# Every fp32r matmul reads and writes its 512 columns in pairs, by turns from the two halves of the row

## The chip, the core and the metric

The kernel runs on one core of a Trainium2 chip. TensorE (PE) multiplies, VectorE (DVE) and ScalarE (ACT) do the elementwise work, GpSimd (POOL) and SyncE (SP) mostly issue DMAs. The time is that of the whole program on the device, in microseconds (us).

## The reference

One transformer block with an FNet mixing layer and a feed-forward layer, S = 2048 rows, D = 512, F = 1792, all fp32:

```python
def _A_ref(x, dft_seq_re, dft_seq_im, dft_hid_re, dft_hid_im):
    a = jnp.einsum("bsd,ed->bse", x, dft_hid_re)
    b = jnp.einsum("bsd,ed->bse", x, dft_hid_im)
    return jnp.einsum("ts,bse->bte", dft_seq_re, a) - jnp.einsum("ts,bse->bte", dft_seq_im, b)

def _B_ref(x, w1, w2):
    h = _silu(jnp.einsum("bsd,df->bsf", x, w1))
    return jnp.einsum("bsf,fd->bsd", h, w2)

h = x + _A_ref(_layernorm(x), ...)
out = h + _B_ref(_layernorm(h), w1, w2)
```

## The kernel before

Every product is made of fp32r matmuls. An fp32 operand is rounded into a high part (on ScalarE, line 266) and a remainder (on VectorE, line 270 or 272), and one product of a weight block with a moving row takes three matmuls: high by high, high by remainder, remainder by high. That is the function `three`, lines 314 to 318. Each of these matmuls loads 128x128 weights, streams 512 moving columns past them and adds the 128x512 result to half of a double PSUM bank (`banks`, two rows of 512 fp32). The moving operand is always one row of 512 fp32r per partition, the high or the low half of a page in SBUF.

The stages, in order: `plain` (the first sequence products, with `L513`, `L515` and `L517` for the first quarter, where the three kinds of matmul are grouped over four blocks), `fast` (the other sequence products, in Strassen-Winograd form with seven products per 2x2 blocks), `mix_fast` (the hidden products), `up` (first feed-forward matrix, with SiLU behind it) and `down` (second feed-forward matrix). Tiles are called ph and pl (parts of the sequence matrices and of mixed blocks), X and S (parts of the normalized input and its sums, which are the weights of the first stages), T1 to T7, gth and gtl (parts of activations), hf, sf, wf, wah, wal (weights).

The order of all instructions is written out ahead of time: each piece of work is an event with a planned time (`step` for matmuls, `at` for others), shifted by a table `MOVED`, and the sorted list fixes the order on every engine. The plan counts `MM_US = 0.2265` for a matmul, prepares remainders `PREP_US = 8` us and loads tiles `LOAD_US = 18` us ahead of their matmul; the waits themselves are semaphores, so that a plan which is off moves the order and not what waits for what. Twelve bf16 matmuls (line 1357) warm TensorE up at the start. They are written apart from `three`.

Of the kernel before, what the change touches and what calls it, by code (L numbers as in the profile page):

```python
# [206 lines left out]
def fnet_ffn_kernel(  # L207
# [18 lines left out]
    for plan.now, *_, f in program(stub, plan.page, stub, stub, stub, stub, x, xT, seq, hid, ffn, out):  # L226
        f()
    places = plan.places()

    def page(name, dt=F32, shape=(2, 512)):  # L230
        return pages.tile([P, *shape], dt, tag=f"pg{next(places)}", name=name)

    events = program(nc, page, keep, small, psum, dram, x, xT, seq, hid, ffn, out)


# [12 lines left out]
def program(nc, page, keep, small, psum, dram, x, xT, seq, hid, ffn, out):  # L248
# [11 lines left out]
    def banks(name):  # L260
        return psum.tile([P, 2, 512], F32, tag="ps", name=name)
# [43 lines left out]
    def newton(v, t, a, b):  # L305
# [5 lines left out]
            nc.vector.tensor_tensor(v, v, t, op=ALU.mult)  # L311
        nc.vector.scalar_tensor_tensor(b, v, 1.5, a, op0=ALU.add, op1=ALU.mult)

    def three(acc, wh, wl, mh, ml, first, last, on=False):

        nc.tensor.matmul(acc, wh, mh, start=first, stop=False, skip_group_check=on)  # L316
        nc.tensor.matmul(acc, wh, ml, start=False, stop=False, skip_group_check=on)  # L317
        nc.tensor.matmul(acc, wl, mh, start=False, stop=last, skip_group_check=on)  # L318

    events, clock = [], [0.0]  # L320

# [116 lines left out]
    raw, part, acc, C = {}, {}, {}, {}  # L438
# [56 lines left out]
    def plain(c, q):  # L495


        def mul(jj, k, tau, tiles, parts):
            hi, lo = parts
            if not acc:  # L500
                for v in ((1, 1), (0, 0), (1, 0), (0, 1)):
                    acc[c, q, *v] = banks(f"c{c}{q}{v[0]}{v[1]}")
            for a in tiles:
                todo = []
                for i in range(2):
                    w = X[i, k, jj]
                    for m in range(2):
                        d = slice(m * P, (m + 1) * P)
                        todo.append((acc[c, q, i, tau][:, m, :], w[:, 0, a, d], w[:, 1, a, d], hi[:, a, :], lo[:, a, :]))
                first, last = jj == 0 and k == 0 and a == 0, jj == 1 and k == 1 and a == 1  # L510
                if jj == 0 and tau == 0:
                    for o, wh, _, mh, _ in todo:
                        nc.tensor.matmul(o, wh, mh, start=first, stop=False)  # L513
                    for o, wh, _, _, ml in todo:
                        nc.tensor.matmul(o, wh, ml, start=False, stop=False)  # L515
                    for o, _, wl, mh, _ in todo:
                        nc.tensor.matmul(o, wl, mh, start=False, stop=last)  # L517
                else:
                    for v in todo:
                        three(*v, first, last)  # L520
# [22 lines left out]
        for a in range(2):  # L543
            step(24, lambda a=a: [mul(0, 0, tau, [a], part[key]) for tau, key in enumerate(keys)])
# [32 lines left out]
        for jj, k, tau in [(jj, k, tau) for jj in range(2) for k in range(2) for tau in range(2)][2:]:  # L577
            key = ("A", c, q, jj, k, tau)
            before = [(LOAD_US, lambda jj=jj, k=k, tau=tau, key=key: load_seq(c, q, jj, k, tau, key)),
                      *halves(PREP_US, lambda key=key: round_raw(key))]  # L580
            if k == 0 and tau == 0:
                before += tiles_x(jj)
            after = [(0, lambda: copy_out("22", acc.pop((c, q, 1, 1))))] if (jj, k, tau) == (1, 1, 1) else []
            step(24, lambda jj=jj, k=k, tau=tau, key=key: mul(jj, k, tau, (0, 1), part.pop(key)), before, after)
# [5 lines left out]
        def prod(n, jj):  # L590
            hi, lo = part.pop(("A", c, q, n, jj))
            w = X[(*A[n], jj)]
            if (n, jj) in ((1, 2), (7, 2)):
                acc[n] = banks(f"c{n}")
            o = acc[{2: (c, q, 0, 0), 3: (c, q, 0, 1), 4: (c, q, 1, 0), 7: 7}.get(n, 1)]
            fresh = n in (1, 7)
            for m in range(2):
                for a in range(2):
                    d = slice(m * P, (m + 1) * P)
                    three(o[:, m, :], w[:, 0, a, d], w[:, 1, a, d], hi[:, a, :], lo[:, a, :],  # L600
                          fresh and jj == 2 and a == 0, jj == 3 and a == 1, not fresh)
# [62 lines left out]
    def fast(c, q):  # L664
# [4 lines left out]
        def mul(n, jj, on=False):  # L669
            hi, lo = part.pop(("A", c, q, n, jj))  # L670
            w = X[(*A[n], jj)]
            for m in range(2):
                for a in range(2):
                    d = slice(m * P, (m + 1) * P)
                    three(acc[c, q, n][:, m, :], w[:, 0, a, d], w[:, 1, a, d], hi[:, a, :], lo[:, a, :],
                          jj == JJ[0] and a == 0 and not on, jj == JJ[-1] and a == 1, on)
# [717 lines left out]
```

## Time and profile before

| | |
|---|---|
| median of 3 runs | 666.58 us (666.52 to 734.88) |
| the profiled execution, its own time | 665.71 us |
| its span, first to last instruction | 663.9 us |
| PE busy, matmuls | 657.9 us, 2892 |
| VectorE busy | 575.6 us |
| ScalarE busy | 371.7 us |
| DMA | 184.22 MB, mean 277 GB/s |

Times in the profile are from the span's start. PE is the stream of matmuls, PEld the weight loads, which run beside it. Matmuls overlap each other (the next one starts while the last columns of the one before are still on their way), so the busy time of one says less than the distance from start to start. PEclk is the clock granted to TensorE, in tenths of full speed. A line like `4.89 0.81 PE L1357 ... x3` in the timeline is a start, the time from the first start to the last end, and how many instructions were put together.

### The profile page before, as it was taken

What the parts mean: (1) busy time and instruction counts of PE and PEld (TensorE: products, weight loads), DVE (VectorE), ACT (ScalarE), POOL (GpSimd) and SP (SyncE); (2) the same over time, 40 slices, a digit from 0 to 9 for tenths busy, and PEclk for the clock granted to TensorE, in tenths of its full rate; (3) what the DMA queues carried; (4) which work ended last, traced back from release to release, by engine and by line L of the source; (5) the groups of instructions that cost most, each with busy time, mean ns of one, the idle gap of its engine ahead of it and who ended that gap; (6) DMA issues with size and microseconds to landing.
All of it is one profiled execution on the core that took longest, in us unless ns stands there. A gap on an engine that the chain in (4) does not pass through costs nothing.

```text
span 663.9 us, 8288 instructions
## 1 busy us (share of the span) xinstructions
PE 657.9 (99%) x2892; PEld 541.9 (82%) x2892; DVE 575.6 (87%) x727; ACT 371.7 (56%) x476; POOL 99.4 (15%) x131
## 2 busy tenths in 40 slices
PE   9999999999999999999999999999999999999997
PEld 5888888888888888888888888888888888888885
DVE  7999989898988999989999998988998854379974
ACT  6997456664445435365674555778543555664600
POOL 0011011112003433111121005343010000000000
PEclk9999999999999999999999999999999999999999
DMA  8982899999799586999999987668979663278803
GB/s 324 370 224 48 269 353 370 313 298 302 268 363 364 165 295 127 397 330 397 322 323 412 408 321 270 237 222 315 342 276 376 226 227 118 80 258 305 324 32 128
DMA packets 59706, 184.22 MB, mean 277 GB/s; under 512 B 6800, under 2 KB 13840, under 8 KB 59664
## 3 DMA queue, kind: packets, MB, share of 16 engines
q1 hardware_dynamic: 45024, 131.22, 54.9%
q0 software_dynamic: 14352, 52.20, 24.6%
q8 instruction: 23, 0.38, 0.3%
q10 hardware_dynamic: 288, 0.26, 0.1%
q14 instruction: 19, 0.16, 0.1%
HBM read 139.34 MB, written 44.32 MB: 277 GB/s over the span
## 4 chain that ended last, share of the span: by engine, by line
PE 98%; DMA 0%; DVE 0%; ACT 0%; issue 0%; DVEq 0%
PE m L318 11%; PE m L316 11%; PE m L317 11%; PE y L318 8%; PE y L317 8%; PE y L316 8%; PE f L318 6%; PE f L317 6%; PE f L316 6%; PE c L317 4%; PE c L316 4%; PE c L318 4%; PE vx L318 3%; PE vx L317 3%; PE vx L316 3%; PE c L517 1%
## 5 line engine op out<-in xcount | busy, mean ns | idle before, releaser
L266 ACT ACTIVATE ph<-raw 128x1024 fp32r<-128x1024 f32 x102 | 106.0, 1057 | 86.7 <-PE m L318 18.6
L270 DVE TENSOR_TENSOR pl<-raw,ph 128x1024 fp32r<-128x1024 f32 x88 | 112.1, 1289 | 8.9 <-ACT ph L266 6.8
L316 PE MATMUL m<-ph,S 128*128 128x512 f32 x192 | 74.7, 389 | 0.0
L317 PE MATMUL m<-pl,S 128*128 128x512 f32 x192 | 74.7, 389 | 0.0
L318 PE MATMUL m<-ph,S 128*128 128x512 f32 x192 | 74.7, 389 | 0.0
L316 PE MATMUL f<-gth,wf 128*128 128x512 f32 x161 | 62.6, 389 | 0.0
L317 PE MATMUL f<-gtl,wf 128*128 128x512 f32 x161 | 62.6, 389 | 0.0
L318 PE MATMUL f<-gth,wf 128*128 128x512 f32 x161 | 62.6, 389 | 0.0
L266 ACT ACTIVATE gth<-g 128x1024 fp32r<-128x1024 f32 x42 | 42.6, 1052 | 32.6 <-DVE g L1208 31.6
L270 DVE TENSOR_TENSOR gtl<-g,gth 128x1024 fp32r<-128x1024 f32 x42 | 50.3, 1218 | 7.0 <-ACT gth L266 5.7
L316 PE MATMUL m<-ph,X 128*128 128x512 f32 x144 | 56.0, 389 | 0.0
L317 PE MATMUL m<-pl,X 128*128 128x512 f32 x144 | 56.0, 389 | 0.0
L318 PE MATMUL m<-ph,X 128*128 128x512 f32 x144 | 56.0, 389 | 0.0
L1079 DVE TENSOR_TENSOR g<-vx,g 128x512 f32<-128x512 f32 x28 | 19.3, 689 | 30.5 <-PE vx L318 17.9
L714 DVE TENSOR_TENSOR raw<-raw,raw 128x1024 f32<-128x1024 f32 x36 | 43.9, 1221 | 0.5
L316 PE MATMUL y<-ph,hf 128*128 128x512 f32 x112 | 43.6, 389 | 0.0
L317 PE MATMUL y<-pl,hf 128*128 128x512 f32 x112 | 43.6, 389 | 0.0
L318 PE MATMUL y<-ph,hf 128*128 128x512 f32 x112 | 43.6, 389 | 0.0
L317 PEld LDWEIGHTS m<-pl,S 128*128 128x128 f32 x192 | 36.1, 188 | 7.5
L318 PEld LDWEIGHTS m<-ph,S 128*128 128x128 f32 x192 | 36.0, 188 | 7.5
L316 PEld LDWEIGHTS m<-ph,S 128*128 128x128 f32 x192 | 36.0, 188 | 7.4
L317 PEld LDWEIGHTS f<-gtl,wf 128*128 128x128 f32 x161 | 30.2, 188 | 6.3
(408 smaller groups left out, 1541.8 us busy)
## 6 DMA issues: line engine op xcount, KB each, us to landing
raw<-in_seq SPq DMA_DIRECT2D x84, 512.0 KB, 7.4
hf<-fd SPq DMA_DIRECT2D x28, 512.0 KB, 7.6
wf<-wd SPq DMA_DIRECT2D x28, 512.0 KB, 5.8
wf<-wd SPq DMA_DIRECT2D x28, 384.0 KB, 5.5
sf<-sd SPq DMA_DIRECT2D x18, 512.0 KB, 5.3
raw<-in_seq POOLq DMA_DIRECT2D x16, 512.0 KB, 7.1
fd<-hf POOLq DMA_DIRECT2D x14, 512.0 KB, 7.3
w<-in_ffn SPq DMA_DIRECT2D x23, 256.0 KB, 5.3
```

The costliest lines, as they stand in the source:

```text
L266: nc.scalar.activation(hi, src, AF.Copy, scale=sign)
L270: nc.vector.tensor_tensor(lo, src, hi, op=ALU.subtract)
L316: nc.tensor.matmul(acc, wh, mh, start=first, stop=False, skip_group_check=on)
L317: nc.tensor.matmul(acc, wh, ml, start=False, stop=False, skip_group_check=on)
L318: nc.tensor.matmul(acc, wl, mh, start=False, stop=last, skip_group_check=on)
L517: nc.tensor.matmul(o, wl, mh, start=False, stop=last)
L714: nc.vector.tensor_tensor(o, a, b, op=ALU.subtract)
L1079: nc.vector.tensor_tensor(g[q, f][:, tau, :], src, g[q, f][:, tau, :], op=ALU.add)
```

## The change

All matmuls but the warm-up go through a helper that hands TensorE both the moving row and the result with their columns in another order: a row of 512 is seen as two halves of 256, each half as 128 pairs, and the order is pair 0 of the first half, pair 0 of the second half, pair 1 of the first half, and so on. The result is addressed in the same order, so that each column ends where it was before. Weights, DMAs, the elementwise work, the plan and its table are as they were.

```diff
+    def turned(columns):
+        return columns.rearrange("p (a t r) -> p t a r", a=2, r=2)
+
+    def mul_add(acc, w, m, **flags):
+
+        nc.tensor.matmul(turned(acc), w, turned(m), **flags)
+
     def three(acc, wh, wl, mh, ml, first, last, on=False):
 
-        nc.tensor.matmul(acc, wh, mh, start=first, stop=False, skip_group_check=on)
-        nc.tensor.matmul(acc, wh, ml, start=False, stop=False, skip_group_check=on)
-        nc.tensor.matmul(acc, wl, mh, start=False, stop=last, skip_group_check=on)
+        mul_add(acc, wh, mh, start=first, stop=False, skip_group_check=on)
+        mul_add(acc, wh, ml, start=False, stop=False, skip_group_check=on)
+        mul_add(acc, wl, mh, start=False, stop=last, skip_group_check=on)
...
                     for o, wh, _, mh, _ in todo:
-                        nc.tensor.matmul(o, wh, mh, start=first, stop=False)
+                        mul_add(o, wh, mh, start=first, stop=False)
                     for o, wh, _, _, ml in todo:
-                        nc.tensor.matmul(o, wh, ml, start=False, stop=False)
+                        mul_add(o, wh, ml, start=False, stop=False)
                     for o, _, wl, mh, _ in todo:
-                        nc.tensor.matmul(o, wl, mh, start=False, stop=last)
+                        mul_add(o, wl, mh, start=False, stop=last)
```

## The prediction

> **What bounds the kernel now.** I read the page first, then the chain that ended last, then the matmuls one by one in the timeline.
>
> ```profile
> span 663.9 us, 8288 instructions
> PE 657.9 (99%) x2892; PEld 541.9 (82%) x2892; DVE 575.6 (87%) x727; ACT 371.7 (56%) x476; POOL 99.4 (15%) x131
> PEclk9999999999999999999999999999999999999999
> PE 98%; DMA 0%; DVE 0%; ACT 0%; issue 0%; DVEq 0%
> L316 PE MATMUL m<-ph,S 128*128 128x512 f32 x192 | 74.7, 389 | 0.0
> L270 DVE TENSOR_TENSOR pl<-raw,ph 128x1024 fp32r<-128x1024 f32 x88 | 112.1, 1289 | 8.9 <-ACT ph L266 6.8
> ...
> 6.02:659.45 653.43, 653.40 (x2880) 540.38 (x2880) 572.83 (x716) 368.83 (x470) 99.15 (x126) 1.00 0.80 279
> ```
>
> PE is busy for 99% of the span, 98% of the chain is PE, and the granted clock is at its highest mark in all slices. So the kernel is its own matmuls in a row. The last line is one stretch, from the first matmul of real work to the end of the last: PE is busy 653.40 of 653.43 us with 2880 of them (the other 12 of the 2892 are the warm-up). Their 389 ns overlap, so the price of one is the step from start to start: (653.43 - 0.16) / 2880 = 0.2268 us, where 0.16 is the part of the last one's 0.389 that nothing follows. Of the span's rest, 6.0 us lie ahead of the stretch and 4.5 behind it.
>
> A price per matmul can come from three places: the weight load, the stream of the moving columns with its results, or work of others that gets in the way. The timeline weighs them.
>
> ```profile
> start us, us, engine line op out<-in xcount [idle before <-releaser]
> 4.89 0.81 PE L1357 MATMUL idle<-warm 128*128 128x512 bf16 x3
> 8.13 0.50 PE L517 MATMUL c<-ph,X 128*128 128x512 f32 x1
> 8.47 0.40 PE L517 MATMUL c<-ph,X 128*128 128x512 f32 x1
> ...
> 8.13 0.19 PEld L517 LDWEIGHTS c<-ph,X 128*128 128x128 f32 x1 [0.45 <-DVE X L409]
> 8.24 0.19 PEld L517 LDWEIGHTS c<-ph,X 128*128 128x128 f32 x1
> ...
> 9.16 0.39 PE L316 MATMUL c<-ph,X 128*128 128x512 f32 x1
> 9.39 0.40 PE L317 MATMUL c<-pl,X 128*128 128x512 f32 x1
> 9.63 0.39 PE L318 MATMUL c<-ph,X 128*128 128x512 f32 x1
> ...
> 13.72 1.07 PE L517 MATMUL c<-ph,X 128*128 128x512 f32 x4
> ...
> L1357 PE MATMUL idle<-warm x12: 379/634/634, 1.2 to 5.3; 128*128 128x512 bf16 x12
> ```
>
> The weight load first. At 8.13 PE had run dry, and a load begins together with its matmul. The next load, which begins when a matmul begins to stream, is at 8.24, and the next matmul at 8.47, one step (0.23) behind that. So a load holds its own matmul up by 0.11 us when nothing covers it; in the steady stream it has a whole step of 0.227 for that. It isn't the bound, by my reading of this one gap.
>
> The stream is. Four matmuls of L517 in 1.07 us give (1.07 - 0.389) / 3 = 0.227 a step. The three last warm-up matmuls, as many columns and as large a result but bf16 on the moving side and in the weights, give (0.81 - 0.379) / 2 = 0.216. The result side is alike in both (512 fp32 columns), so the 0.011 us between them belong to the operands: to the moving columns, twice as wide, or to the weights. The rows can't part these two, and that is the main doubt below.
>
> Other engines' work: the steps stay as they are whether the rest is busy or not.
>
> ```profile
> core 0: us, PE busy (x) PEld busy (x) DVE busy (x) ACT busy (x) POOL busy (x), PEclk, DMA share, GB/s
> 25.00:50.00 25.00, 25.00 (x112) 20.68 (x112) 24.47 (x45) 24.18 (x35) 3.58 (x4) 1.00 0.92 258
> 50.00:75.00 25.00, 25.00 (x112) 20.72 (x111) 24.90 (x34) 15.78 (x22) 1.69 (x2) 1.00 0.46 126
> 125.00:150.00 25.00, 25.00 (x112) 20.70 (x111) 23.92 (x26) 16.00 (x21) 4.79 (x8) 1.00 0.93 279
> 225.00:250.00 25.00, 25.00 (x112) 20.72 (x111) 24.48 (x32) 9.08 (x12) 8.01 (x7) 1.00 0.75 230
> 250.00:275.00 25.00, 25.00 (x112) 20.72 (x111) 24.57 (x24) 13.40 (x15) 9.15 (x9) 1.00 0.76 223
> 300.00:325.00 25.00, 25.00 (x112) 20.72 (x111) 24.16 (x29) 14.64 (x17) 5.03 (x8) 1.00 1.00 355
> 325.00:350.00 25.00, 25.00 (x112) 20.72 (x111) 24.93 (x29) 17.36 (x19) 5.72 (x10) 1.00 1.00 341
> 350.00:375.00 25.00, 25.00 (x112) 20.71 (x111) 24.79 (x28) 11.97 (x14) 1.07 (x2) 1.00 1.03 409
> 375.00:400.00 25.00, 25.00 (x112) 20.69 (x111) 24.51 (x29) 12.88 (x16) 2.15 (x4) 1.00 0.90 335
> 475.00:500.00 25.00, 25.00 (x112) 20.72 (x111) 24.62 (x41) 13.72 (x15) 3.26 (x6) 1.00 0.86 300
> 550.00:575.00 25.00, 25.00 (x112) 20.69 (x111) 12.29 (x16) 13.75 (x24) 0.53 (x1) 1.00 0.33 111
> ```
>
> From 325 to 350 us DVE and the DMA engines are full, from 550 to 575 they are at half and at a third, and PE goes through 112 matmuls in both. Only at the very start are there slower steps: 9.16 to 9.63 holds two of 0.235.
>
> **The change, part by part.** Nothing is removed, added or moved: 2880 matmuls, 2880 weight loads, the same DMAs, the same waits. The same column j of the moving row still goes to column j of the result, so evictions and their readers see what they saw. What changes is the order of columns in one matmul: 0, 1, 256, 257, 2, 3, 258, 259, and so on, on both sides. The 12 warm-up matmuls and all weights stay as they are. So the sum has one term, 2880 x (new step - 0.2268), plus whatever comes late when PE gets quicker.
>
> The trace holds no strided matmul, so the new step is bounded by the nearest rows. From below: the bf16 step, 0.216, which has half the bytes on the moving side. From above: a row read in pairs by turns comes back to every stretch of it twice. Cut in pieces of four columns (two neighbouring pairs, which the turns part), the row today takes 128 visits in 0.2268 us, 1.77 ns each; in pairs it takes 256, and if each costs as much, the step is 0.454. Between ends this far apart I take the lower one, 0.216. The reasons are the two facts above: the result side doesn't set the step, and the extra 0.011 stands with operands that are twice as wide. A limit on how fast one place can deliver wide columns is eased when consecutive pairs come from two places 1 KB apart. That is an inference and not a row. It is the nearer end too, 0.011 off against 0.227.
>
> [...]
>
> The gain by the lower end: 2880 x (0.2268 - 0.216) = 31.1 us.
>
> What is late next: 25 us of today's matmuls would take 25 x 0.216 / 0.2268 = 23.81 us. In ten of the windows above, all but the last, DVE has more work than that; the sum of its busy times there is 245.35, and 245.35 - 238.1 = 7.2 us. PE would wait for DVE's remainders (L270, 1.2 us each) by up to that much. Remainders are planned 8 us ahead of their matmul and quieter stretches lie between, so I charge half, 3.6 us. The DMA engines are at 1.00 or over from 300 to 375 us: three windows short by 1.19 each, 3.6 us at most. I charge nothing for them, because loads are planned 18 us ahead, and keep it for the range.
>
> The sum: 665.7 (the profiled execution's own time, 1.8 us more than its span) - 31.1 + 3.6 = 638.2. The median of the runs, 666.58, lies 0.9 above the profiled time, which gives **639**. Its own range: at the low end the bf16 step read at its rounding, 0.215, with no late DVE: 665.7 - 34.0 + 0.9 = 632.6; at the high end 31.1 gained, 7.2 and 3.6 lost: 646.3, and some more for a step that only comes near 0.216: 650.
>
> **The rivals.**
>
> *The step stays.* The 0.011 us come from the weights, not from the moving columns: fp32 loads take 0.19 us, and a fixed part of each may hold the stream up. For it: the step is the same to the last digit over tiles, stages and load on memory, which looks like something fixed in the instruction. Against it: the uncovered load held its matmul up by 0.11 only, and 0.19 ends before the next step. The change then does what it says to the order and nothing to the time: 666. An order that costs a little and wins a little also ends here.
>
> *Slower: each pair is a visit of its own.* Place: the read of the moving row, or the write of the results. Price: p ns a visit, 256 visits a matmul. It decides from p = 0.2268 / 256 = 0.886 ns, below which the visits hide behind the present step. At 0.92 the step is 0.2355, as in the two steps at 9.16, and the time 666.6 + 2880 x 0.0087 = 692. At the full 1.77 it is 0.454, and 666.6 + 2880 x 0.2268 = 1320. For it: such slower steps at the start show that the stream can be held up. Against it: no strided row of the trace, and the result side isn't the limit today. Nothing covers such a loss, because PE has no idle time; DVE, ACT and DMA would only get more slack. [...]
>
> **How the numbers follow.** What can be told from no change here is about 2%, 653 to 680 us. The forecast, 632 to 650, gets 0.43. The step that stays gets 0.28. Slower gets 0.29: about 0.10 for a price per visit just past the deciding point, up to 695, and 0.19 for prices beyond, anywhere up to 1320. A range of 632 to 695 then holds 0.43 + 0.28 + 0.10 = 0.81. The likeliest case's own range, 632 to 650, holds less than half, since cases of both signs weigh much.
>
> **What would show it.** Count the steps in the timeline: matmuls of L316 to L318 0.216 apart instead of 0.227 show the first term right; with it, idle time of PE in front of matmuls that read a `pl` or `gtl` tile, released by DVE L270, between 300 and 400 us shows the second. Steps of 0.227 with PE at 99% show the first rival. Longer steps, the same in quiet and in busy windows and with no idle time on PE, show the second, and their length divided by 256 is its price. I'm wrong by far if the visits cost what they cost today.

## The result: every matmul became longer by 0.1 us

The changed kernel takes 972.58 us (median of 6 runs, 957.86 to 991.8) where the kernel before takes 666.26, which is 1.46 times as long. The ratio with an interval, 1.4487 (95%: 1.434 to 1.4634), counts only the executions of 957.86 and 972.15 us, because the other four are over 1.5% longer than the shortest. The profiled execution is the shortest, 957.86 us. The head of its page:

```profile
span 956.1 us, 8297 instructions
PE 950.8 (99%) x2892; PEld 566.2 (59%) x2892; DVE 577.0 (60%) x727; ACT 373.0 (39%) x476; POOL 97.3 (10%) x131
PEclk9999999999999999999999999999999999999999
```

PE is still busy all the time at the full granted clock, and the other engines do as many instructions in the same busy time as before (DVE 577.0 against 575.6). Only their share fell. PE waits for nothing new; the matmuls are longer. The timeline of PE at both ends (start, time to the last end, what) gives the step:

```profile
5.92 1.73 PE L319 MATMUL c<-ph,X 128*128 128x512 f32 x4
...
951.43 0.50 PE L319 MATMUL f4b<-gth,wf 128*128 128x512 f32 x1
```

From the first start to the last there are 2879 steps: (951.43 - 5.92) / 2879 = 0.3284 us, where it was 0.2268. The sum closes: 2880 x 0.1016 = 292.6 us, and the spans differ by 956.1 - 663.9 = 292.2. The step doesn't care for what goes on around it (busy times by stretch):

```profile
466.00:491.00 25.00, 25.00 (x78) 14.93 (x77) 15.61 (x21) 10.66 (x12) 2.54 (x4) 1.00 0.74 220
790.00:815.00 25.00, 25.00 (x78) 14.94 (x77) 8.15 (x10) 9.77 (x17) 0.53 (x1) 1.00 0.20 73
```

78 matmuls touch each of the two windows of 25 us, with the DMA engines at 0.74 and at 0.20 and with VectorE at 62% and at 33%. And where VectorE was the busiest engine behind PE before, it now waits for its inputs: ScalarE sits until a matmul frees its page, and VectorE sits for ScalarE (who waited for whom, 300 to 400 us; total, times, longest).

```profile
ACT ph L266 <- PE m L319: 43.1, 14, 7.7
DVE pl L270 <- ACT ph L266: 17.0, 8, 5.7
```

### The profile page after: what moved, and what is told of

Same layout as the page of the kernel before. It is cut to its first block, busy times and chain, and to the rows that moved or that the text cites. A ratio compares the mean times of both kernels' runs of the same rounds, so it can differ in the third digit from the quotient of the medians.

```text
span 956.1 us, 8297 instructions
## 1 busy us (share of the span) xinstructions
PE 950.8 (99%) x2892; PEld 566.2 (59%) x2892; DVE 577.0 (60%) x727; ACT 373.0 (39%) x476; POOL 97.3 (10%) x131
## 4 chain that ended last, share of the span: by engine, by line
PE 99%; DVE 0%; ACT 0%; issue 0%
PE m L319 35%; PE y L319 23%; PE f L319 19%; PE c L319 12%; PE vx L319 8%; PE f4b L319 1%; PE idle L1364 1%; PE x L319 0%; DVE r L1272 0%; ACT r L1270 0%; DVE warm L1355 0%; DVE upper L1357 0%; DVE lower L1356 0%
## 5 line engine op out<-in xcount | busy, mean ns | idle before, releaser
L266 ACT ACTIVATE ph<-raw 128x1024 fp32r<-128x1024 f32 x102 | 105.6, 1052 | 155.1 <-PE m L319 117.0
L319 PE MATMUL m<-ph,S 128*128 128x512 f32 x384 | 162.8, 506 | 0.0
L319 PE MATMUL m<-pl,S 128*128 128x512 f32 x192 | 97.2, 506 | 0.0
L319 PEld LDWEIGHTS f<-gth,wf 128*128 128x128 f32 x322 | 63.1, 196 | 42.6
L319 PE MATMUL f<-gtl,wf 128*128 128x512 f32 x161 | 81.5, 506 | 0.0
L319 PEld LDWEIGHTS m<-ph,X 128*128 128x128 f32 x288 | 56.4, 196 | 38.2
L319 PE MATMUL m<-pl,X 128*128 128x512 f32 x144 | 72.9, 506 | 0.0
L319 PE MATMUL c<-ph,X 128*128 128x512 f32 x176 | 72.1, 507 | 0.0
L319 PEld LDWEIGHTS y<-ph,hf 128*128 128x128 f32 x224 | 43.9, 196 | 29.6
L319 PE MATMUL y<-pl,hf 128*128 128x512 f32 x112 | 56.7, 506 | 0.0
L319 PEld LDWEIGHTS c<-ph,X 128*128 128x128 f32 x176 | 34.6, 196 | 23.3 <-issue 0.3
L319 PEld LDWEIGHTS f<-gtl,wf 128*128 128x128 f32 x161 | 31.6, 196 | 21.3
```

Of the source, the lines that this page charges most:

```text
L266: nc.scalar.activation(hi, src, AF.Copy, scale=sign)
L319: nc.tensor.matmul(turned(acc), w, turned(m), **flags)
```

## Experiments

### Which side pays: the read

The turns are put on one side only, in the whole kernel.

```diff
-        nc.tensor.matmul(turned(acc), w, turned(m), **flags)
+        nc.tensor.matmul(acc, w, turned(m), **flags)      # read only
+        nc.tensor.matmul(turned(acc), w, m, **flags)      # write only
```

> The changed kernel with the turns on the moving rows alone, results written straight (its results therefore stand in another order of columns and are not the reference's). READ: about 958 us, as with both. WRITE: 666 us. RUN: 958 if the two sides hide each other. Adding up: about 812.

> The changed kernel with the turns on the results alone, moving rows read straight (results in another order of columns, not the reference's). READ: 666 us. WRITE: about 958. RUN: 958. Adding up: about 812.

Turns on the read alone: 972.27 us, ratio 1.4591 (1.4559 to 1.4622). Turns on the write alone: 666.38 us, ratio 1.0004 (0.9995 to 1.0014). PE's lines of the two pages, read first:

```profile
PE 964.6 (99%) x2892; PEld 563.0 (58%) x2892; DVE 576.6 (59%) x727; ACT 373.9 (39%) x476; POOL 97.5 (10%) x131
...
PE 659.0 (99%) x2892; PEld 542.5 (82%) x2892; DVE 575.5 (87%) x727; ACT 371.6 (56%) x476; POOL 99.6 (15%) x131
```

The whole loss is on the side of the moving columns. Writing the results in turned pairs costs nothing measurable here.

### What it pays for: patterns side by side

A block of probe matmuls, 24 of a kind on one page of constant data, goes in front of the kernel's work, behind the warm-up; the work itself is as before.

```diff
+    words = page("words", F32R)          # 0.5 everywhere
+    def turned(columns, r, a=2):
+        return columns.rearrange("p (a t r) -> p t a r", a=a, r=r) if r else columns
+    def probe(name, read, write, ...):
+        bank = banks(name)[:, 0, :]
+        for k in range(24):
+            nc.tensor.matmul(turned(bank, write), words[:, 1, :P], turned(words[:, 0, :], read), ...)
```

> The kernel before with a block of probe matmuls put in front of its work, 24 of each kind on one page of constant fp32r data, 512 columns: moving row and result straight; in turns of 2, 4 or 8 columns on both sides, on the read alone or on the write alone; single columns by turns on the read; pairs taken with every second one left for a second sweep (skip), read or write; and three kinds that add to the result instead of starting it. Straight should give 0.227 us a step, pairs on both sides 0.328, as in the two kernels. Theory READ (each pair is a visit of its own to the moving row, about 1.28 ns): pairs on the read 0.328, pairs on the write 0.227, fours and eights 0.227 everywhere, skipped pairs on the read 0.328, single columns on the read about 0.65. Theory WRITE (the results pay): pairs on the write 0.328, on the read 0.227, skipped pairs on the write 0.328. Theory RUN (each new run of an access pattern costs a fixed time on whichever side, 0.101 us for 256 runs): pairs 0.328 on both sides alone, fours 0.277, eights 0.252. A fourth way out, both sides adding up: pairs on each side alone near 0.277.

One row of the timeline is one kind. The distance from a row's start to the next row's, divided by 24, is the step.

```profile
5.92 6.43 PE L1373 MATMUL straight<-words 128*128 128x512 f32 x24
12.19 8.32 PE L1373 MATMUL pairsBoth<-words 128*128 128x512 f32 x24
20.33 8.33 PE L1373 MATMUL pairsRead<-words 128*128 128x512 f32 x24
28.49 5.64 PE L1373 MATMUL pairsWrite<-words 128*128 128x512 f32 x24
33.97 6.17 PE L1373 MATMUL foursBoth<-words 128*128 128x512 f32 x24
39.98 6.17 PE L1373 MATMUL foursRead<-words 128*128 128x512 f32 x24
45.98 5.65 PE L1373 MATMUL foursWrite<-words 128*128 128x512 f32 x24
...
57.30 6.00 PE L1373 MATMUL eightsRead<-words 128*128 128x512 f32 x24
63.14 5.61 PE L1373 MATMUL eightsWrite<-words 128*128 128x512 f32 x24
68.59 5.34 PE L1373 MATMUL onesRead<-words 128*128 128x512 f32 x24
73.77 11.00 PE L1373 MATMUL skipRead<-words 128*128 128x512 f32 x24
84.59 5.65 PE L1373 MATMUL skipWrite<-words 128*128 128x512 f32 x24
90.07 5.60 PE L1373 MATMUL straightAdd<-words 128*128 128x512 f32 x24
95.51 8.32 PE L1373 MATMUL pairsReadAdd<-words 128*128 128x512 f32 x24
```

Straight 0.227, by the row `straightAdd`; the row `straight`, right behind the warm-up, took 0.8 us more (6.43 against 5.60). Pairs by turns on the read 0.340, on both sides 0.339, on the write 0.228. Runs of 4 on the read 0.250, of 8 0.243. Pairs with every second one left for a second sweep ("skip"), 0.451. And single columns by turns from the two halves, of which I expected 0.65: **0.216**, less than straight.

So READ holds and WRITE falls. RUN falls too, since runs on the write cost nothing and the price isn't proportional to the number of runs (256 runs 0.113 more than straight, 128 runs 0.023, 64 runs 0.017). READ's own figures held for the pairs and the writes alone: it had runs of 4 and 8 free, skipped pairs at 0.328 and singles at 0.65. The skipped pairs come to 0.451 / 256 = 1.76 ns a visit, the price of the prediction's upper end; pairs by turns come to 1.28 to 1.33.

The whole kernel with runs of 4 on both sides (`r=4` for `r=2`) agrees with its probe:

> The changed kernel with runs of 4 columns in place of 2, on both sides. By the probe's 0.2498 a step for runs of 4: 666.3 + 2880 x 0.0231 = 733 us, with PE busy all the time and steps of about 0.25 in all windows. If the cost of the pairs had been only that 16 bytes are visited twice, runs of 4 would cost nothing: 666.

It took 732.83 us, against 733 worked out from the probe.

### Other widths, other sizes

> The same block with other kinds, 24 of each: bf16 rows (0.5 everywhere) straight, in pairs on both sides, on the read, on the write, fours and eights on the read, fours on the write; 384 and 256 columns in bf16 and in fp32r; fp32r pairs by turns at 384 and 256 columns; fp32r pairs by turns from four quarters of the row, read or write. If the read pays by visits of a fixed stretch of bytes, bf16 pairs on the read pay too, bf16 eights not. If the write pays, bf16 pairs on the write step as slowly as fp32r ones, about 0.32. Quarters like halves (0.328) if it is the visit, another time if it is the distance. On the 0.011 us between bf16 (0.216) and fp32r (0.227): if it comes from the moving columns it shrinks with them, fp32r 384 at 0.170 and 256 at 0.113; if it is fixed per weight load, 0.173 and 0.120.

```profile
5.77 5.34 PE L1373 MATMUL bfStraight<-warm 128*128 128x512 bf16 x24
10.95 6.67 PE L1373 MATMUL bfPairsBoth<-warm 128*128 128x512 bf16 x24
17.45 6.67 PE L1373 MATMUL bfPairsRead<-warm 128*128 128x512 bf16 x24
23.96 5.34 PE L1373 MATMUL bfPairsWrite<-warm 128*128 128x512 bf16 x23
29.14 5.60 PE L1373 MATMUL bfFoursRead<-warm 128*128 128x512 bf16 x24
34.58 5.34 PE L1373 MATMUL bfEightsRead<-warm 128*128 128x512 bf16 x24
39.76 5.34 PE L1373 MATMUL bfFoursWrite<-warm 128*128 128x512 bf16 x23
44.94 4.06 PE L1373 MATMUL bfShort<-warm 128*128 128x384 bf16 x24
48.84 2.78 PE L1373 MATMUL bfHalf<-warm 128*128 128x256 bf16 x24
51.38 4.43 PE L1373 MATMUL short<-words 128*128 128x384 f32 x24
55.64 3.03 PE L1373 MATMUL half<-words 128*128 128x256 f32 x24
58.51 4.16 PE L1373 MATMUL halfPairsRead<-words 128*128 128x256 f32 x24
62.49 3.05 PE L1373 MATMUL halfPairsWrite<-words 128*128 128x256 f32 x24
65.38 6.09 PE L1373 MATMUL shortPairsRead<-words 128*128 128x384 f32 x24
71.30 10.83 PE L1373 MATMUL quartersRead<-words 128*128 128x512 f32 x24
81.94 5.64 PE L1373 MATMUL quartersWrite<-words 128*128 128x512 f32 x24
```

In the rows with x23 one record is missing; 24 matmuls ran. In bf16, straight and every write 0.216, pairs on the read 0.271, fours 0.227, eights (16 bytes) 0.216. Turned bf16 pairs pay on the read as well, less than fp32r ones. With fp32r pairs from two halves the price goes with their number: 0.166 at 256 columns and 0.247 at 384, which is 1.30 and 1.29 ns for each pair. The places matter too: the same 256 pairs taken by turns from four quarters of the row step at 0.443, or 1.73 ns each (on the write 0.228). Whether the number of places does that or their distance, 128 columns, isn't parted here. But the length and the number of the runs alone don't set the price. By the starts of the rows, straight fp32r took 0.120 at 256 columns and 0.178 at 384, bf16 0.106 and 0.163. The 0.120 is the figure of a fixed cost, 0.178 is above both of mine; what fp32r takes over bf16, 0.011 at 512 columns, was 0.015 at 384 and 0.014 at 256, so it didn't shrink with the row. By my own condition that spoke for the weights; the single columns, with the same weights and no such 0.011, say that the moving side can do without it. That condition was badly chosen: a cost of the moving side may be fixed per matmul.

### Why singles are quick: not settled

> A block of probe matmuls like the two before, now with single columns by turns on the read and straight results (24 of each): from 2 halves, 4 quarters, 8, 16, 32 parts of the row, every eighth, every fourth, every second column (which are 64, 128 and 256 parts); halves once more adding to the result, with pairs on the write, with 384 and with 256 columns; bf16 straight, bf16 single columns from halves, bf16 every second column; fp32r straight. Single columns from halves gave 0.216. Theory PLACES (two places 1 KB apart relieve each other, and only neighbours in one place are slow): parts that lie near each other, every second column (8 bytes apart) above all, go back to 0.227 or more. Theory SINGLE (a run of one column is fetched in another way than a run of two or more, whatever the distance): 0.216 in all of them, and bf16 singles too. Theory LINE (a stretch of 16 bytes costs 1.77 ns each time it is visited anew): every fourth column and wider would need 0.9, every second 0.45.

```profile
10.95 6.95 PE L1373 MATMUL quartersRead<-words 128*128 128x512 f32 x24
17.74 11.90 PE L1373 MATMUL eighthsRead<-words 128*128 128x512 f32 x24
29.46 10.58 PE L1373 MATMUL sixteenthsRead<-words 128*128 128x512 f32 x24
...
60.61 11.22 PE L1373 MATMUL everyFourthRead<-words 128*128 128x512 f32 x24
71.65 11.01 PE L1373 MATMUL everySecondRead<-words 128*128 128x512 f32 x24
82.48 5.36 PE L1373 MATMUL halvesAddRead<-words 128*128 128x512 f32 x24
87.68 5.34 PE L1373 MATMUL halvesReadPairsWrite<-words 128*128 128x512 f32 x24
...
104.63 11.79 PE L1373 MATMUL bfHalves<-warm 128*128 128x512 bf16 x24
116.25 5.58 PE L1373 MATMUL bfEverySecond<-warm 128*128 128x512 bf16 x24
```

In fp32r only two streams are quick: halves 0.217 or less, quarters 0.283, eighths 0.488, every fourth column 0.460, every second 0.451. In bf16 it is the other way round: singles from halves 0.484, every second column 0.226 ((5.58 - 0.379) / 23, where 0.379 is the time of one bf16 matmul in the kernel before). SINGLE falls. PLACES has columns that lie near each other slow, as they are, but nothing in it makes the eighths (64 columns apart) slower than every second column, or pairs from the two halves slow. LINE has the every second column right (0.45) and falls with every fourth (0.9 expected) and with the halves, which it would make as slow. The last theory, about the distance of the two streams:

> A block of probe matmuls again, results straight, 512 columns read by turns from two streams that lie 256, 258, 260, 264, 272, 288, 320, 384 or 512 columns (of 4 bytes) apart: single columns, then pairs. At 256 singles gave 0.216 and pairs 0.340. Theory DISTANCE (streams collide where their places agree in some address bits, so 1 KB apart is special): singles lose their 0.216 at some distances, and pairs reach 0.227 or less at some. Theory RUN (only the length of the run matters): singles 0.216 and pairs 0.33 to 0.34 at every distance.

```profile
47.94 5.34 PE L1378 MATMUL ones_512x<-words 128*128 128x512 f32 x24
53.12 8.32 PE L1378 MATMUL pairs_256x<-words 128*128 128x512 f32 x24
61.27 8.11 PE L1378 MATMUL pairs_258x<-words 128*128 128x512 f32 x24
69.21 8.01 PE L1378 MATMUL pairs_260x<-words 128*128 128x512 f32 x24
77.06 8.01 PE L1378 MATMUL pairs_264x<-words 128*128 128x512 f32 x24
...
108.58 8.17 PE L1378 MATMUL pairs_384x<-words 128*128 128x512 f32 x24
```

Singles stay at 0.216 to 0.217 at every distance tried (258 to 512 columns here, 256 in the first block), pairs at 0.327 to 0.340. DISTANCE falls: no distance takes the 0.216 from the singles or brings the pairs near 0.227. Its part in the pairs' step is small at most: 0.340 at 256 columns, 0.331 at 258, 0.327 from 260 to 288, 0.333 at 320 and 384. Measured is that two streams of single fp32r columns are read without the cost of the straight row and two streams of pairs with much more; no theory here gives both, and why stays open.

### Single columns in the whole kernel

> The changed kernel with single columns by turns from the two halves on the read (runs of 1 in place of 2) and results written straight; the results stand in another order of columns and are not the reference's. If the 0.216 of the probe holds in the whole kernel: 2880 x 0.011 = 31.6 us less than before, 635 us, plus up to 7 us in which VectorE is late, so 635 to 642. If the probe's step only holds in a quiet core, 666 or more. If the read of single columns is hurt by transfers and other engines: a step that differs between busy and quiet windows.

```diff
-        return columns.rearrange("p (a t r) -> p t a r", a=2, r=2)
+        return columns.rearrange("p (a t) -> p t a", a=2)
-        nc.tensor.matmul(turned(acc), w, turned(m), **flags)
+        nc.tensor.matmul(acc, w, turned(m), **flags)
```

649.64 us, ratio 0.976 (0.9743 to 0.9776). Faster, but only by 16 of the 31.6 us that the step promises. The page's engines, then PE's longest wait:

```profile
PE 630.9 (97%) x2892; PEld 544.0 (84%) x2892; DVE 574.7 (89%) x727; ACT 370.6 (57%) x476; POOL 99.4 (15%) x131
...
PE m L319 <- DVE pl L270: 4.6, 4, 1.5
```

PE's idle time grew from 663.9 - 657.9 = 6.0 to 647.6 - 630.9 = 16.7 us, with VectorE's remainders first: 4.6 us for this `pl`, 1.1 for a `gtl` and 0.5 for another `pl`, 6.2 in all. That is the late VectorE of the prediction, above its 3.6 and below its upper bound of 7.2. The step itself is 0.216 where PE doesn't run dry: 116 matmuls touch the 25 us from 425, and 234 the 50 us from 550, where the kernel before has 112 in 25 us. Of the 15 us that are missing from the gain, 10.7 are PE's idle time; the others lie in its busy time, which fell by 27.0 and not by 31.6.

Three ways of mending the order follow.

> The whole kernel with single columns by turns on the read and straight results, and the order of columns mended, so that it computes the reference: the sequence matrices and two arrays come in another order of columns from the host, and the rounding operations of the feed-forward stages read every second column first. Against the same order unmended (649.6 us) nothing is added but the stride of 8 bytes in 56 pairs of rounding operations on ScalarE and VectorE. If that stride is free: 649 to 651 us. If such an operation takes half as long again, 0.6 us more on VectorE each, most of it in stages where VectorE has room: up to 660. If it takes twice as long, the gain is gone: 666 or more.

```diff
+        src, hi, lo = src.rearrange("p b (t a) -> p b a t", a=2), ...   # in rounded(), up and down stages
         nc.scalar.activation(hi, src, AF.Copy, scale=sign)
+    seq, xT and the result in another order of columns on the host
```

667.18 us, ratio 1.0023 (1.0012 to 1.0035): the gain is gone. Groups by form, and PE's longest wait:

```profile
L275 ACT ACTIVATE gth<-g 128x1024 fp32r<-128x1024 f32 x42 | 62.8, 1542 | 28.9 <-DVE g L1225 26.8
L279 DVE TENSOR_TENSOR gtl<-g,gth 128x1024 fp32r<-128x1024 f32 x42 | 60.5, 1467 | 9.3 <-ACT gth L275 9.3
...
PE f L328 <- DVE gtl L279: 7.8, 5, 3.1
```

The rounding on ScalarE takes 1542 ns against 1052 straight, the remainder on VectorE 1467 against 1218, and PE waits for it.

> Single columns by turns on every read, results straight, order mended in another place: the host gives the sequence matrices and two arrays in another order as before, and only the 14 pairs of rounding operations at the start of the two up stages read every fourth column first, which makes up for up and down together; the 42 + 14 pairs in the down stages stay straight. The windows from 500 us on should lose the waits for gtl (7.8 us in the mended kernel before this one) and look as in the unmended one; near 400 us one to four us of waits for T tiles are left. So 651 to 656 us, against 649.6 unmended and 667.2 mended in every rounding. If the stride of 16 bytes makes one such operation twice as long or worse, the 14 pairs alone cost up to 8 us: 660. 666 or more would mean that the gain doesn't survive any mending.

673.56 us, ratio 1.0108 (1.009 to 1.0126), though only 14 pairs of operations are strided here. The edit is `a=4` in place of `a=2`, in the rounding at the start of `up` alone. The first of them, and a stretch behind it:

```profile
L275 ACT ACTIVATE T1h<-hn x2: 2933/2942/2952, 352.6 to 519.7; 128x1024 fp32r<-128x1024 f32 x2
L279 DVE TENSOR_TENSOR T1l<-hn,T1h x2: 2899/2903/2907, 358.3 to 522.6; 128x1024 fp32r<-128x1024 f32 x2
...
350.00:400.00 50.00, 41.83 (x179) 34.71 (x178) 47.84 (x43) 31.74 (x24) 2.17 (x4) 0.93 0.84 323
```

With a stride of 16 bytes these two take 2.9 us each, more than twice the straight ones; on ScalarE the roundings of the other T tiles take 2.07 (T6h) to 2.97 (T5h), 1.05 to 1.06 in the kernel before. PE is busy for 41.83 of the 50 us, and the granted clock is at 0.93 in that window. My bound for "worse" was 660. It counted the operations' own time alone, and PE's two longest waits, 5.7 us for a `pl` and 4.1 for `wal`, are for other operations of VectorE. That these came late because strided ones stood ahead of them is my reading; no view here shows it.

> Single columns by turns on the read only in the sequence and hidden stages (about 1700 of the 2880 matmuls), straight reads in the up and down stages; the order is mended on the host alone (sequence matrices, one array in, the result out), with no strided operation on ScalarE or VectorE. It computes the reference. 1706 x 0.011 = 18.7 us from the steps; in the unmended kernel some 12 us of waits (mostly for VectorE and for tiles it frees) came back in these stages, so about 660 us, 658 to 662. If those waits came from the later stages running ahead too, less of them: down to 650. If nothing is left of the gain here: 666.

```diff
+    def mul_add(acc, w, m, straight=False, **flags):
+        nc.tensor.matmul(acc, w, m if straight else m.rearrange("p (a t) -> p t a", a=2), **flags)
...     up and down call three(..., straight=True); seq, xT and the result reordered on the host
```

660.62 us, ratio 0.9926 (0.9912 to 0.994), with 660 expected. With the order mended on the host alone this one beats both kernels, the one before by 0.7%.

## Why the prediction was wrong

**Held.** PE bounds the kernel and nothing covers a longer step: all of the 292 us went into the span. The sum has one term, the step. The weight load isn't the bound (the same loads stand beside single columns at 0.216), and the result side isn't: turned writes 0.228. The extra 0.011 us of fp32r can be had back on the moving side, with the same weights: 0.216, the very end that I took. VectorE is late next when the step gets there: 6.2 us of waits for it with single columns.

**Failed.** The choice between the ends of the step: the term of -31.1 us measured +292. I took 0.216 because consecutive pairs "come from two places 1 KB apart" and would ease a limit, an inference that no row showed. The runs show that two places don't ease the read of pairs (0.327 to 0.340 at nine distances, 0.328 in the kernel) and that four places make it dearer still (0.443). The end that I took belongs to another pattern, single columns from two places (0.216 at nine distances). The row nearest to the new pattern in the trace was not the bf16 step but the price of a visit, 1.77 ns, and the calculation of 256 visits was at hand. "Nearer by numbers" (0.011 against 0.227) was no reason: it measured how far the ends are from today, not which of them resembles the change. The upper end wasn't right either: 0.328 lies about halfway between 0.216 and 0.454, and no row of the trace before gave that.

**The rivals.** The one that held is the second, a price for each pair, with its place on the read; the price is about the same for 128, 192 and 256 pairs from two halves (1.28 to 1.33 ns). 1.28 ns in the changed kernel lies between its deciding point 0.886 and its upper end 1.77, which the skipped pairs reach (1.76). Its chance, 0.29, was too low, and I put a third of that into a narrow strip just past the deciding point, to which the range then reached; the range ended at 695. As a rule it is too simple, though: at 1.28 ns it would let runs of 4 go free (128 visits, 0.164 us; 0.250 measured), single columns by turns would cost most, and pairs from four places no more than from two (0.443 measured). The first rival, a step fixed by the weights, falls by the single columns.

**Open.** Executions of the changed kernel spread from 958 to 992 us with the granted clock at 0.999 or 1.0 in all six; the kernel before, at 0.998 or more, keeps to 665.6 to 666.8. Profiles have three steps for pairs by turns: 0.328 in the changed kernel, 0.333 with turns on the read alone, 0.340 in the first probe. Times of 972 and 992 us would fit the latter two (958 + 2880 x 0.005 and 0.0116), but what sets the step of an execution is not known. The last probe block has the same three steps in one execution, from one distance to another. Nor is it shown what in the read costs the time: every matmul here has a weight load of its own beside it, and no run parts the read of the moving columns from its meeting with that load.

## What to carry to other kernels

The order in which the moving columns are read is part of a matmul's price. Against one contiguous run (0.227 us for 512 fp32r columns), short runs by turns from two halves cost up to half as much again (0.340), and several other orders cost about twice as much (0.431 to 0.488). In the changed kernel the step was the same in a busy and in a quiet window (78 matmuls in 25 us, with the DMA engines at 0.74 and at 0.20). Put patterns of one side alone into a probe block of two dozen matmuls before changing a kernel; one run prices sixteen of them. Where a step's price lies between two far ends, ask which end's row does what the new instruction does, and let the range reach to the other.

## What the runs showed that I had not expected

Single fp32r columns by turns from two streams are read at 0.216 us a matmul, 0.011 below the straight row, at nine distances from 1 to 2 KB; from four streams it is 0.283 and in bf16 0.484. Pairs by turns read from four quarters of the row step at 0.443, from two halves at 0.327 to 0.340. Turned pairs on the result cost nothing (666.38 us against 666.07). A rounding that reads SBUF with a stride of 16 bytes took 2.07 to 2.97 us on ScalarE and 2.9 (T1l) on VectorE, against 1.05 and 1.22 straight.
